# A linear-attention and MLP kernel: seven block products for one more group, 100 unread matmuls at the start, and casts moved between engines

## The chip, the cores and the metric

The kernel runs on one core of a Trainium2 chip. A core has TensorE for matrix products, VectorE, ScalarE and GpSimd for elementwise work, and SyncE (SP), which here only issues transfers. Each engine takes its own instructions in order, and they wait for each other by semaphores. The metric is the device time of one execution in microseconds; less is better.

## The reference

Two layers follow each other. The first is attention with a decaying state, in blocks of 64 positions, for 4 sequences of 768 positions and 8 heads of 64. Its output is normalised and goes through an MLP with a residual:

```python
for b in range(nb):
    intra = np.einsum('bhic,bhjc->bhij', qb, kb) * Dmask[None]
    intra = np.einsum('bhij,bhjd->bhid', intra, vb)
    inter = np.einsum('bhid,bhde->bhie', qb * lam_pow[None], kv_state)
    out[:, :, sl] = intra + inter
    kv_state = lam_block * kv_state + np.einsum('bhsd,bhse->bhde', kb * rev_pow[None], vb)
...
xn = (x - mu) / np.sqrt(var + 1e-06) * g_ln
ch = np.maximum(xn @ w_ch1, 0.0) @ w_ch2          # 512 -> 2048 -> 512
return (x + ch).astype(np.float32)
```

## The kernel before

The 3072 positions are cut into 12 units of 256, each a pair of two chunks of 128 of one sequence. Units 0 to 3 are the first 256 positions of the four sequences, 4 to 7 the next, 8 to 11 the last. Unit u has its attention, and then the MLP for its two tiles of 128 positions, which make group u. The order of all work is written out by hand at the end of the kernel: the attention's steps are called by name, and between them `units(n)` takes the next n pieces of MLP work from a list, `plan`. A piece of the first layer (`m1`, line 530) is eight 128x256 matmuls.

Input stage. `load_in` and `load_window` issue the transfers of k, q and v on SP, `load_w1` and `load_w2` those of the weights, in four pieces each, on GpSimd's queue. `behind` (line 727) makes GpSimd read one column of a tile, so that the weight transfers issued after it start only when that tile has landed; in the same way `open_in(u, True)` writes one column of k's buffer on GpSimd ahead of that unit's loads. `in_k` and `in_k_one` cast k to bf16, `in_q` and `in_q_one` scale q, `in_v` scales v; each call names its engine. The transposes of k and q are TensorE's (`transpose_pe`, line 250) for units 0 to 2 and transfers (`transpose_dma`, line 257) for the later ones.

Attention. `scores` and `mask` make the masked products of k and q, `kv` the state products pk0 and pk1 in PSUM (line 307), `new_state` adds the old state on VectorE (`Stmp`, line 317) and multiplies by the decay on GpSimd (`Sn`, line 313), `av` and `inter` sum the output in PSUM. `s1` is `kv`, `scores`, `new_state` and `mask` together; `s2` is the second half of the scores; `X1` and `X2` are the like for the later units. `reader` (line 443) copies eight columns of the output's PSUM as a fence between the two halves of `inter`; the constant WG decides its engine. `norm` takes the mean and makes xc; g_row in it is the norm's weight, which one matmul with a row of ones (`g_all`, line 180) spreads over 128 partitions. `to_xT` transposes xc.

Second layer. For groups below WG = 4 it is the plain product (`m2`, line 666): for each of two tiles 16 matmuls of 128x512. For groups from WG on it is a scheme with seven products in place of eight (`m2.w`, line 565): the operands are cut 2 x 2, sums of blocks are made beforehand, and each product is eight matmuls of 128x256. The weights' block sums `wt` are made once (`w_sums(c, n)`, two VectorE operations for each half n of piece c, 16 in all), those of the hidden layer for each group (`sums`, lines 548 to 550, six VectorE operations). The products accumulate in four PSUM tiles, a to d, taken from the same four buffers ("mm") as pm1, pk0 and pk1:

```python
        products = (("P1", "a", True), ("P2", "b", True), ("P7", "c", True), ("P5", "d", True),
                    ("P6", "a", False), ("P4", "c", False), ("P3", "d", False))
```

`evict` takes them out: P1 and P7 through ScalarE (`ev_u`, `ev_p`) and an add on GpSimd (lines 590 and 598), the others on VectorE (line 578). Each `m2.w` piece is seven matmuls, so that a group's second layer is eight pieces either way.

Of the kernel before, what the change touches and what calls it, by code (L numbers as in the profile page):

```python
# [7 lines left out]
F32 = mybir.dt.float32  # L8
BF16 = mybir.dt.bfloat16
# [8 lines left out]
def kernel(  # L18
# [11 lines left out]
    nc = tc.nc  # L30
# [11 lines left out]
    NWC = 4  # L42
    eps = 1e-6
    XS = 64.0
    WG = 4
    assert D == 64 and S % W == 0 and DM == 512

    ctx.enter_context(tc.manual_schedule())
# [1 line left out]
    const = ctx.enter_context(tc.tile_pool(name="const", bufs=1))  # L50
# [4 lines left out]
    ps = ctx.enter_context(tc.tile_pool(name="ps", bufs=1, space=PSUM))  # L55
# [16 lines left out]
    def fill(got, name, u, hs, eng=None):  # L72
        eng = eng or nc.sync
        src = dict(k=k, q=q, v=v)[name]
        if u < LB:
            eng.dma_start(got[:, hs], source(src, u, hs))
            return
        cc, b = divmod(u, B)
        for j in range(2):
            eng.dma_start(got[:, hs, j * D:(j + 1) * D],  # L80
                          src[b, hs, cc * W + j * C:cc * W + (j + 1) * C, :].rearrange("h p d -> p h d"))
# [11 lines left out]
    def load_in(u, name, eng):  # L93
        got = qkv_in[u][name]
        fill(got, name, u, slice(0, H), eng)
        qkv_in[u][name] = got.rearrange("p h (j d) -> p h j d", j=2)
# [28 lines left out]
    g_row = const.tile([128, DM], F32)  # L125
    g_one = wk.tile([1, DM], F32, tag="xc", name="g_one")
    nc.scalar.dma_start(g_one, moe_g_ln[None, :])


    ident = const.tile([128, 128], BF16)  # L130
# [20 lines left out]
    def make_keep64():  # L151
        for dst, base in ((keep64, 0), (keep64_b, D)):
            nc.gpsimd.memset(dst, 1.0)
            nc.gpsimd.affine_select(
                out=dst, in_=dst, compare_op=ALU.is_ge, fill=0.0,
                base=base, pattern=[[1, D]], channel_multiplier=-1,
            )
        nc.vector.tensor_copy(keep64[half[1]], keep64_b[half[1]])
# [18 lines left out]
    ones = const.tile([1, 128], F32)  # L177
    nc.vector.memset(ones, 1.0)
    g_all = ps.tile([128, DM], F32, tag="po1", name="g_all")
    nc.tensor.matmul(g_all, lhsT=ones, rhs=g_one, start=True, stop=True)  # L180

    lnlam = const.tile([128, H], F32)
# [15 lines left out]
    def open_window(u):  # L198
        kq = wk.tile([128, 2, NP, 2, 2, D], BF16, tag="kq", bufs=3, name="kq")
        vb = wk.tile([128, H, 2, D], BF16, tag="vb", bufs=4, name="vb")  # L200
        st[u] = dict(kq=kq, vb=vb)
        if u < XB:
            st[u]["kqT"] = wk.tile([128, 2, NP, 2, 128], BF16, tag="kqT", bufs=3, name="kqT")

    def part(a, dst, hs):

        return dst[:, a, hs.start // 2:hs.stop // 2].rearrange("p a j e d -> p a e j d")
# [3 lines left out]
    def in_k(u, eng, hs=ALL):  # L211
        src = qkv_in[u]["k"][:, hs].rearrange("p (a e) j d -> p a e j d", e=2)
        dst = part(0, st[u]["kq"], hs)
        for j in range(2):
            (eng.copy if eng is nc.scalar else eng.tensor_copy)(dst[:, :, :, j], src[:, :, :, j])
# [13 lines left out]
    def in_k_one(u, eng, j):  # L229
        src = qkv_in[u]["k"].rearrange("p (a e) j d -> p a e j d", e=2)  # L230
        (eng.copy if eng is nc.scalar else eng.tensor_copy)(part(0, st[u]["kq"], ALL)[:, :, :, j], src[:, :, :, j])

    def in_q_one(u, eng, j):
        src = qkv_in[u]["q"].rearrange("p (a e) j d -> p a e j d", e=2)
        lq = (lam_q[:, :, j] if u < LB else lam_p[:, 0, :]).rearrange("p (a e) -> p a e", e=2)
        eng.tensor_tensor(part(1, st[u]["kq"], ALL)[:, :, :, j], src[:, :, :, j],  # L236
                          lq[:, :, :, None].to_broadcast([128, NP, 2, D]), op=ALU.mult)
# [22 lines left out]
    def scores(u, hf, early=False):  # L260

        s = st[u]
        kT, qT = s["kqT"][:, 0], s["kqT"][:, 1]
        if early:
            sc = [mm_tile([128, 2, 2, 128], F32, f"sce{e}") for e in range(2)]
        else:
            sc = [ps.tile([128, 2, 2, 128], F32, tag="sc", bufs=2, name=f"sc{e}") for e in range(2)]
        mA = wk.tile([128, 2, 2, 2, 128], BF16, tag=f"mA{hf}", name=f"mA{hf}")
        for i in range(2):
            for jk in range(2):  # L270
                for ab in range(2):
                    for e in range(2):
                        nc.tensor.matmul(sc[e][half[ab], i, jk, :], lhsT=kT[half[e], 2 * hf + i, jk, half[ab]],  # L273
                                         rhs=qT[half[e], 2 * hf + i, :, half[ab]],
                                         start=(i == 0 and jk == 0), stop=(i == 1 and jk == 1), skip_group_check=True)
        s[f"mA{hf}"] = mA
        s[f"sc{hf}"] = sc

    def mask(u, hf, heads=(0, 1)):
        s = st[u]  # L280
        kp = keep.rearrange("p a b t -> p a (b t)")
        for e in heads:
            nc.vector.tensor_tensor(s[f"mA{hf}"][:, e], s[f"sc{hf}"][e],  # L283
                                    kp[:, None, :, :].to_broadcast([128, 2, 2, 128]), op=ALU.mult)
# [139 lines left out]
    def inter(u, first, fence=True):  # L424


        s = st[u]
        qT = s["kqT"][:, 1]
        todo = [(e, p, ab, jq) for p in range(NP) for jq in range(2)
                for e, ab in ((first, 0), (1 - first, 1)) if s["S"][ab][jq] is not None]  # L430
        for i, (e, p, ab, jq) in enumerate(todo):
            nc.tensor.matmul(s["po"][ab][half[jq], 2 * p + e, :], lhsT=qT[half[e], p, jq, half[ab]],  # L432
                             rhs=s["S"][ab][jq][half[e], p, :],
                             start=False, stop=(first == 1 and i >= len(todo) - 4), skip_group_check=True)
        if first == 0 and fence:
            reader(u)

    def reader(u):
        s = st[u]
        for ab in range(2):  # L440
            if s["S"][ab][1] is not None:
                seen = wk.tile([128, H], F32, tag="seen", name="seen")
                (nc.scalar.copy if u > WG else nc.vector.tensor_copy)(seen, s["po"][ab][:, :, 0])

    def norm(u, ab, early=False):
        s = st[u]
# [66 lines left out]
    m2s = {}  # L513
# [267 lines left out]
    def w_sums(c, n):  # L781
        v = w2[c].rearrange("p (k e) d -> p k e d", e=2)
        w = DM // 2
        b11, b12, b21, b22 = v[:, :, 0, 0:w], v[:, :, 0, w:], v[:, :, 1, 0:w], v[:, :, 1, w:]
        t1, t2, t3, t4 = (wt[c][:, :, i] for i in range(4))
        if n == 0:
            nc.vector.tensor_tensor(t1, b12, b11, op=ALU.subtract)
            nc.vector.tensor_tensor(t3, b12, b22, op=ALU.add)
        else:
            nc.vector.tensor_tensor(t2, b11, t3, op=ALU.subtract)  # L790
            nc.vector.tensor_tensor(t4, t2, b21, op=ALU.add)
# [28 lines left out]
    def s1(u):  # L820
        kv(u)
        scores(u, 0)
        new_state(u, 0, nc.gpsimd)
        mask(u, 0, (0,))
        new_state(u, 1, nc.gpsimd)
        mask(u, 0, (1,))
# [38 lines left out]
    def s2(u):  # L865
        scores(u, 1)
        mask(u, 1)
# [11 lines left out]
    def s4(u):  # L879
        inter(u, 1)  # L880
        if st[u]["S"][0][1] is not None:
            norm(u, 0)
        norm(u, 1)
# [55 lines left out]


    open_window(1)
    in_k(1, nc.scalar)
    norm(0, 0, early=True)
    reader(0)
    behind(qkv_in[1]["k"][:, 0, 0, 0:1])
# [72 lines left out]
    for g in range(2, len(groups)):  # L1018
        m1, m2 = mlp(g)
        plan += [(m1, n) for n in range(m1.count)]  # L1020
        if g >= WG:
            plan += [(m2.w, n) for n in range(8)]
# [5 lines left out]
    def units(n):  # L1028
        for _ in range(n):
            f, *a = next(steps)  # L1030
            f(*a)
# [15 lines left out]
    s3(2)  # L1047
    units(2)
    s4(2)
    open_window(3)  # L1050
    in_k_one(3, nc.vector, 0)
    in_k_one(3, nc.vector, 1)
    in_q_one(3, nc.gpsimd, 0)
    in_q_one(3, nc.gpsimd, 1)
    in_v(3, nc.gpsimd)
# [10 lines left out]
    units(1)  # L1066
    load_in(5, "v", nc.sync)
    units(1)
    open_window(4)
    in_k_one(4, nc.gpsimd, 0)  # L1070
    in_k_one(4, nc.gpsimd, 1)
# [1 line left out]
    in_q_one(4, nc.gpsimd, 1)  # L1073
    in_v(4, nc.gpsimd)
    units(5)
    w_sums(0, 0)
    w_sums(0, 1)
    units(2)
    w_sums(1, 0)
    units(1)  # L1080
    s1(3)
    store(0)
    transpose_dma(4, 0)
    transpose_dma(4, 1)
    units(2)
    s2(3)
    units(1)
    open_window(5)
    in_k_one(5, nc.gpsimd, 0)
# [8 lines left out]
    open_in(6, False)  # L1098
    load_in(6, "k", nc.sync)
    units(1)  # L1100
    load_in(6, "q", nc.sync)
    units(1)
    w_sums(1, 1)
    load_in(6, "v", nc.sync)
    units(1)
    w_sums(2, 0)
    transpose_dma(5, 0)
    units(1)
    make_keep64()
    to_xT(3, 0)  # L1110
    transpose_dma(5, 1)
    open_in(7, False)
    load_in(7, "k", nc.sync)
    units(1)
    w_sums(2, 1)
    s1(4)
    to_xT(3, 1)
    open_window(6)
# [7 lines left out]
    units(2)  # L1126
    s3(4)
    units(1)
    in_q_one(6, nc.vector, 1)
    in_v(6, nc.gpsimd)  # L1130
    s4(4)
    in_q_one(6, nc.vector, 0)
    units(3)
    load_in(7, "q", nc.sync)
    units(1)
    w_sums(3, 0)
    w_sums(3, 1)
    units(1)
    open_in(8, False)
    to_xT(4, 0)  # L1140
# [216 lines left out]
```

## Time and profile before

| | us |
|---|---|
| median of 7 runs | 210.84 |
| lowest and highest | 209.77, 212.53 |
| the profiled execution | 209.77 |
| its span, first to last instruction | 208.1 |

| engine | busy, us | share of the span |
|---|---|---|
| TensorE | 198.1 | 95% |
| VectorE | 137.7 | 66% |
| ScalarE | 120.0 | 58% |
| GpSimd | 84.8 | 41% |

The profile is one execution; its instructions carry start and length, the line of the kernel, the tiles written and read, and, in brackets, how long the engine was idle before and what ended that. PE is TensorE, PEld its weight loads, DVE VectorE, ACT ScalarE, POOL GpSimd. The ends of matmuls are modelled, so that in a stream their starts, or the chain that ended last, tell the pace. A row "x16" is sixteen instructions merged, with the time from the first start to the last end. The granted clock in this profile is 1.00 throughout. The program moves 36.39 MB by transfers, at a mean of 175 GB/s.

### The profile page before, as it was taken

What the parts mean: (1) busy time and instruction counts of PE and PEld (TensorE: products, weight loads), DVE (VectorE), ACT (ScalarE), POOL (GpSimd) and SP (SyncE); (2) the same over time, 40 slices, a digit from 0 to 9 for tenths busy, and PEclk for the clock granted to TensorE, in tenths of its full rate; (3) what the DMA queues carried; (4) which work ended last, traced back from release to release, by engine and by line L of the source; (5) the groups of instructions that cost most, each with busy time, mean ns of one, the idle gap of its engine ahead of it and who ended that gap; (6) DMA issues with size and microseconds to landing.
All of it is one profiled execution on the core that took longest, in us unless ns stands there. A gap on an engine that the chain in (4) does not pass through costs nothing.

```text
span 208.1 us, 7231 instructions
## 1 busy us (share of the span) xinstructions
PE 198.1 (95%) x3099; PEld 156.1 (75%) x3099; DVE 137.7 (66%) x277; ACT 120.0 (58%) x277; POOL 84.8 (41%) x116
## 2 busy tenths in 40 slices
PE   2989999999999999999999999999999999999992
PEld 0468788555775587488888888888888888988881
DVE  2677570529565767767888776676877947865253
ACT  3865769235354667357566775585596565652620
POOL 4649138239556330635365441782282202011020
PEclk9999999999999999999999999999999999999999
DMA  4999999999999988984897999798957020178403
GB/s 109 299 269 217 209 298 168 226 305 263 194 317 191 217 188 160 194 249 78 184 212 116 189 199 167 198 217 129 230 107 175 3 50 3 25 144 274 119 14 88
DMA packets 91042, 36.39 MB, mean 175 GB/s; under 512 B 65153, under 2 KB 88193, under 8 KB 91010
## 3 DMA queue, kind: packets, MB, share of 16 engines
q1 hardware_dynamic: 86400, 31.53, 72.3%
q0 software_dynamic: 4224, 4.19, 12.5%
q8 instruction: 24, 0.39, 0.8%
q10 hardware_dynamic: 386, 0.20, 0.4%
q14 instruction: 8, 0.07, 0.1%
HBM read 27.27 MB, written 6.29 MB: 161 GB/s over the span
## 4 chain that ended last, share of the span: by engine, by line
PE 78%; issue 7%; DVE 5%; ACT 4%; DMA 3%; POOL 1%; SPq 1%; POOLq 0%; ACTq 0%; DVEq 0%
PE pm L530 31%; PE pm L666 14%; PE pwa L565 5%; PE pwd L565 5%; PE pwc L565 5%; PE pwb L565 3%; PE pm1t L640 2%; PE po L419 2%; PE po L432 2%; DMA out_dram<-x 2%; PE sc L273 1%; DMA g_one<-in_moe_g_ln_dram 1%; PE tp L250 1%; PE xt L493 1%; DVE x L578 1%
## 5 line engine op out<-in xcount | busy, mean ns | idle before, releaser
L530 PE MATMUL pm<-xT,w 128*128 128x256 bf16 x736 | 84.8, 273 | 0.0
L530 PEld LDWEIGHTS <-w 128*128 128x128 bf16 x736 | 70.5, 98 | 9.5 <-DVE Smid L388 0.3
L533 ACT ACTIVATE hT<-pm 128x512 f16<-128x512 f32 x92 | 53.9, 600 | 29.2 <-PE pm L530 29.1
L666 PE MATMUL pm<-w,hT 128*128 128x512 f16 x128 | 30.2, 380 | 0.0
L565 PEld LDWEIGHTS <-hs 128*128 128x128 f16 x256 | 24.9, 98 | 2.9
L313 POOL TENSOR_TENSOR Sn<-Stmp,lam_s 128x256 bf16<-128x256 f32 x16 | 9.8, 616 | 39.1 <-DVE Stmp L317 21.0
L590 POOL TENSOR_TENSOR x<-ev_u,x 128x256 f32<-128x256 f32 x8 | 6.4, 796 | 46.4 <-ACT ev_u L589 46.4
L548 DVE TENSOR_TENSOR hs<-hT 128x1024 f16<-128x1024 f16 x16 | 13.8, 864 | 16.5 <-ACT hT L533 16.5
L565 PEld LDWEIGHTS <-hT 128*128 128x128 f16 x192 | 18.1, 98 | 3.6 <-ACT hT L533 1.6
L666 PEld LDWEIGHTS <-hT 128*128 128x128 f16 x128 | 11.7, 98 | 12.1
L283 DVE TENSOR_TENSOR mA<-sc,keep 128x512 bf16<-128x512 f32 x20 | 13.1, 685 | 6.6 <-PE sc L273 6.6
L458 ACT ACTIVATE x<-po 128x512 f32<-128x512 f32 x18 | 10.6, 591 | 9.8 <-PE po L419 5.5
L460 DVE SCALAR_TENSOR_TENSOR xc<-po,nmean,g_row 128x512 bf16<-128x512 f32 x18 | 13.0, 746 | 4.5 <-ACT nmean L459 4.4
L503 ACT ACTIVATE sq<-x,nmean 128x512 bf16<-128x512 f32 x18 | 13.0, 721 | 0.3
L578 DVE SCALAR_TENSOR_TENSOR x<-pwd,rstd,x 128x256 f32<-128x256 f32 x16 | 7.7, 483 | 8.0 <-POOL x L598 8.0
L236 POOL TENSOR_TENSOR kq<-qin,lam_q 128x512 bf16<-128x512 f32 x10 | 10.3, 1045 | 6.1 <-DMA qin<-in_q_dram 6.1
L242 POOL TENSOR_TENSOR vb<-vin,lam_p 128x1024 bf16<-128x1024 f32 x6 | 11.4, 1897 | 2.2 <-DMA vin<-in_v_dram 2.2
L242 POOL TENSOR_TENSOR vb<-vin,lam_v 128x1024 bf16<-128x1024 f32 (+1 forms) x7 | 11.8, 1687 | 1.1 <-DMA vin<-in_v_dram 1.1
L550 DVE TENSOR_TENSOR hs<-hs,hT 128x512 f16<-128x512 f16 x16 | 10.1, 628 | 0.6
L494 ACT COPY xT<-xt 128x512 bf16<-128x512 bf16 x10 | 5.8, 584 | 7.7 <-PE xt L493 7.7
L236 POOL TENSOR_TENSOR kq<-qin,lam_p 128x512 bf16<-128x512 f32 x9 | 9.3, 1043 | 1.5 <-DMA qin<-in_q_dram 1.5
L597 ACT ACTIVATE ev_p<-pwc,rstd 128x256 f32<-128x256 f32 x8 | 3.8, 476 | 10.2 <-PE pwc L565 10.2
(129 smaller groups left out, 305.0 us busy)
## 6 DMA issues: line engine op xcount, KB each, us to landing
out_dram<-x SPq DMA_DIRECT2D x22, 256.0 KB, 3.9
w<-in_moe_w_ch_dram POOLq DMA_DIRECT2D x8, 512.0 KB, 8.7
kin<-in_k_dram SPq DMA_DIRECT2D x14, 256.0 KB, 5.2
qin<-in_q_dram SPq DMA_DIRECT2D x14, 256.0 KB, 4.9
vin<-in_v_dram SPq DMA_DIRECT2D x14, 256.0 KB, 5.1
kin<-in_k_dram SPq DMA_DIRECT2D x5, 512.0 KB, 7.1
qin<-in_q_dram SPq DMA_DIRECT2D x5, 512.0 KB, 8.4
vin<-in_v_dram SPq DMA_DIRECT2D x5, 512.0 KB, 8.5
```

The source lines that it names most:

```text
L236: eng.tensor_tensor(part(1, st[u]["kq"], ALL)[:, :, :, j], src[:, :, :, j], lq[:, :, :, None].to_broadcast([128, NP, 2, D]), op=ALU.mult)
L242: eng.tensor_tensor(st[u]["vb"][:, hs], qkv_in[u]["v"][:, hs], lv.to_broadcast([128, n, 2, D]), op=ALU.mult)
L283: nc.vector.tensor_tensor(s[f"mA{hf}"][:, e], s[f"sc{hf}"][e], kp[:, None, :, :].to_broadcast([128, 2, 2, 128]), op=ALU.mult)
L458: nc.scalar.activation(x, po, ACT.Copy, accum_out=sm)
L460: nc.vector.scalar_tensor_tensor(xc, in0=po, scalar=nm, in1=g_row, op0=ALU.add, op1=ALU.mult)
L503: nc.scalar.activation(sq, s["x"][:, ab], ACT.Square, bias=s["nmean"][:, ab:ab + 1], accum_out=ss[:, ab:ab + 1])
L530: nc.tensor.matmul(pm[:, b, :], lhsT=w1[n // W2K][:, kk, (n % W2K) * 128:(n % W2K + 1) * 128], rhs=xT_of[g][:, kk, 0:N], start=(b == 0 and ...
L533: nc.scalar.activation(hT[:, u * NB:(u + 1) * NB, 0:N], pm, ACT.Relu)
L548: nc.vector.tensor_tensor(s13, b[:, :, 1:2, :].to_broadcast([128, n, 2, 128]), b[:, :, 0:4:3, :], op=ALU.subtract)
L550: nc.vector.tensor_tensor(s4, s2, b[:, :, 2], op=ALU.add)
L565: nc.tensor.matmul(pr[bank], lhsT=lhs(r), rhs=rhs, start=(first and r == 0), stop=(r == KB // 2 - 1), skip_group_check=True)
L666: nc.tensor.matmul(acc[i], lhsT=hT[:, kk, i * 128:(i + 1) * 128], rhs=w2[kk // W2K][:, kk % W2K, :], start=(kk == 0), stop=(kk == KB - 1))
```

## The change

- WG goes from 4 to 3: group 3 (the fourth pair's) takes the seven products. The engine of `reader` no longer follows WG: it is ScalarE from unit 3 on, where it was from unit 5 on.
- A tile of zeros, `fill_in`, is set by VectorE as its first instruction, and 100 matmuls of it with itself (8 columns onto 8 partitions, each with its weight load) stand on TensorE ahead of `g_all`. Nothing reads their output.
- The cast of unit 1's k goes from ScalarE to GpSimd, where it stands ahead of `behind` and of the issue of two weight pieces.
- The cast of unit 3's k goes from VectorE to ScalarE, the scaling of unit 6's q from VectorE to GpSimd.
- The eight calls of `w_sums` are spread over earlier places in the order, since group 3 needs all of them, and group 3 gets its two calls of `sums`.

```diff
-    WG = 4
+    WG = 3
...
+    fill_in = const.tile([128, 8], BF16)
+    nc.vector.memset(fill_in, 0.0)
...
     g_all = ps.tile([128, DM], F32, tag="po1", name="g_all")
+    fill_ps = ps.tile([128, 8], F32, tag="po0", name="idle")
+    for _ in range(100):
+        nc.tensor.matmul(fill_ps[0:8], lhsT=fill_in, rhs=fill_in, start=True, stop=True)
     nc.tensor.matmul(g_all, lhsT=ones, rhs=g_one, start=True, stop=True)
...
-                (nc.scalar.copy if u > WG else nc.vector.tensor_copy)(seen, s["po"][ab][:, :, 0])
+                (nc.scalar.copy if u > 2 else nc.vector.tensor_copy)(seen, s["po"][ab][:, :, 0])
...
     open_window(1)
-    in_k(1, nc.scalar)
+    in_k(1, nc.gpsimd)
...
     s4(2)
+    w_sums(0, 0)
     open_window(3)
-    in_k_one(3, nc.vector, 0)
-    in_k_one(3, nc.vector, 1)
+    in_k_one(3, nc.scalar, 0)
+    in_k_one(3, nc.scalar, 1)
...
     load_in(5, "v", nc.sync)
     units(1)
+    w_sums(0, 1)
     open_window(4)
...
     units(5)
-    w_sums(0, 0)
-    w_sums(0, 1)
-    units(2)
     w_sums(1, 0)
-    units(1)
+    w_sums(1, 1)
+    units(3)
     s1(3)
...
     s2(3)
+    w_sums(2, 0)
     units(1)
     open_window(5)
...
     load_in(6, "k", nc.sync)
     units(1)
+    w_sums(2, 1)
     load_in(6, "q", nc.sync)
     units(1)
-    w_sums(1, 1)
     load_in(6, "v", nc.sync)
     units(1)
-    w_sums(2, 0)
+    w_sums(3, 0)
     transpose_dma(5, 0)
     units(1)
+    w_sums(3, 1)
     make_keep64()
...
     units(1)
-    w_sums(2, 1)
     s1(4)
...
-    in_q_one(6, nc.vector, 1)
+    in_q_one(6, nc.gpsimd, 1)
     in_v(6, nc.gpsimd)
     s4(4)
-    in_q_one(6, nc.vector, 0)
-    units(3)
+    in_q_one(6, nc.gpsimd, 0)
+    units(1)
+    m2s[3].sums(0, 4)
+    units(2)
     load_in(7, "q", nc.sync)
     units(1)
-    w_sums(3, 0)
-    w_sums(3, 1)
+    m2s[3].sums(4, 8)
     units(1)
     open_in(8, False)
     to_xT(4, 0)
```

## The prediction

> **What bounds the kernel now.** I read the busy digits first, then the chain that ended last, then the timeline of the stages that the change touches. From the page, the header and two rows of the 40 slices:
>
> ```profile
> span 208.1 us, 7231 instructions
> PE   2989999999999999999999999999999999999992
> DMA  4999999999999988984897999798957020178403
> ```
>
> TensorE is full from about 30 us to the end; the transfers are full from 5 to about 75 us. The chain says what TensorE's time is made of (start, length, what):
>
> ```profile
> 37.61 0.86 PE pm L666 x4
> ...
> 48.84 5.18 PE pm L666 x24
> ...
> 98.63 0.87 PE pwb L565 x8
> 99.51 0.87 PE pwc L565 x8
> ```
>
> In a stream, a 128x512 matmul of the plain second product costs 5.18/24 = 216 ns, a 128x256 one of the seven block products 0.87/8 = 109 ns. Before 30 us it is otherwise. The timeline:
>
> ```profile
> 4.13 2.04 PE L180 MATMUL g_all<-g_one,ones 1*128 1x512 f32 x2 [4.13 <-DMA g_one<-in_moe_g_ln_dram]
> 6.11 0.61 PE L250 MATMUL tp<-ident,kq 128*128 128x128 bf16 x4
> 11.39 0.44 POOL L727 COPY seen_p<-kin 128x1 f32<-128x1 f32 x1 [0.41 <-DMA kin<-in_k_dram]
> 12.49 1.18 ACT L215 CAST kq<-kin 128x512 bf16<-128x512 f32 x2
> 15.84 1.87 PE L640 MATMUL pm1t<-xT,w 128*128 128x128 bf16 x16 [0.32 <-ACT xT L494]
> 18.87 1.05 PE L640 MATMUL pm1t<-xT,w 128*128 128x128 bf16 x16
> 31.86 2.05 POOL L236 TENSOR_TENSOR kq<-qin,lam_q 128x512 bf16<-128x512 f32 x2 [0.82 <-DMA qin<-in_q_dram]
> 33.90 0.63 PE L250 MATMUL tp<-ident,kq 128*128 128x128 bf16 x8
> ```
>
> Two things are to be seen. The same sixteen matmuls take 1.87 us at 15.84 and 1.05 us at 18.87: until about 18 us TensorE runs slow, though the row of the granted clock shows full speed. And at 33.90 the transposes of the third unit's q start as GpSimd ends its scaling (31.86 + 2.05 = 33.91), which began when that q landed. Nothing on TensorE leads to this q: its transfer waited for a GpSimd gate behind the third piece of the first weights (issued at 12.58, 9.9 us to landing, so 22.5), and the gate's other work waits for transfers too. So 33.9 us is a time that TensorE cannot pass however early it comes; behind it TensorE shows next to no idle time up to about 177 us.
>
> **What the Trainium skill says.** "TensorE: Matmul & The Clock Gate", Part 1: the array starts at half clock and goes to full after some 3.4 us of sustained work, in a window that runs free, so that the moment shifts from run to run. The trace agrees: 117 against 66 ns a matmul above. The same page, "Wait — 56ns, not 53.3ns?": a warm matmul takes its columns at 2.4 GHz plus 2.5 ns (the 216 and 109 ns above), and none starts less than 25 ns after the one before; no run here shows the last. "Trainium Architecture — The Big Picture", "What this means for kernel authors": VectorE and GpSimd lock each other out of a shared port. The trace agrees for an operation with two SBUF inputs:
>
> ```profile
> 109.58 1.90 POOL L242 TENSOR_TENSOR vb<-vin,lam_p 128x1024 bf16<-128x1024 f32 x1
> 109.63 2.38 DVE L548 TENSOR_TENSOR hs<-hT 128x1024 f16<-128x1024 f16 x1 [0.75 <-ACT hT L533]
> ```
>
> It takes 0.69 us alone and here ends 0.53 us after GpSimd.
>
> **The change, part by part.**
>
> *Seven products for group 3.* Removed: 32 matmuls at 216 ns = 6.91 us. Added: 56 at 109 ns = 6.11 us. On TensorE, -0.80 us, all of it behind 33.9, where nothing else limits. The price is paid in waits. In the built order of the changed program, the fifth pair's state products (unit 5, s1(5)) come between the second and the third product, and the fourth accumulator takes over the PSUM buffer of pk1, which VectorE frees only with its second Stmp. In before that state product ends at 82.9, and then:
>
> ```profile
> 82.98 0.43 DVE L317 TENSOR_TENSOR Stmp<-pk,Sn 128x256 f32<-128x256 f32 x1 [1.21 <-PE pk L307]
> 83.48 0.61 POOL L313 TENSOR_TENSOR Sn<-Stmp,lam_s 128x256 bf16<-128x256 f32 x1 [7.05 <-DVE Stmp L317]
> 84.13 0.42 DVE L317 TENSOR_TENSOR Stmp<-pk,Sn 128x256 f32<-128x256 f32 x1
> ```
>
> So pk1 is free 1.65 us after the state product ends. TensorE has until then scores 0.35, two matmuls 0.22 and the third product 0.87 = 1.44 us. The fourth waits 0.2 us, plus what GpSimd and VectorE are late: the new GpSimd add of ev_u (0.80) stands ahead of Sn. Its chain: first product ends 1.09 us after the first layer (8 x 0.109 + transposes 0.22), xT copy 0.59, ev_u 0.47, add 0.80: 2.95, against 2.34 + 0.5 for Sn. That is 0.1 us late. Bounds of the wait 0 and 0.7; I take 0.3. Behind the waiting matmul stand only TensorE's own next products. The six sums of this group on VectorE (2 x (0.69 + 0.42 + 0.42) = 3.1 us) take the place of two q scalings (1.22 + 0.68) and four weight sums (1.7) at 76 to 82 us, so they add no load; the last three end at about 82.6, when the first Stmp is due. The evictions grow from two of 0.74 to six on VectorE (3.1 us together), two of 0.47 on ScalarE and two of 0.8 on GpSimd; VectorE is 65% busy from 80 to 90 us and takes the 1.6 us more beside TensorE's work. Net -0.5 (-0.8 to -0.1).
>
> *The weight sums, moved 7 to 15 us earlier, and the operations that make room.* The third pair of casts of k goes to ScalarE (1.1 us from 46.7 on, in an idle time of 1.13; in before VectorE needs 2.63 us there, locked out by GpSimd). The sums at 61.7 stand against GpSimd's scaling and can be locked out up to 3 us; VectorE's next due work is xc at 64.0, used at 67.5, so this is covered. Unit 6's q goes to GpSimd, 2.1 us in gaps (it idles 2.17 before 74.54 and from 76.4 to 83.5). The readers (0.24 us) go to ScalarE, idle there. On SP the transposes of unit 3 come 2 us sooner, and the loads behind them. All nothing; if the cover failed, up to 0.5 us at one place.
>
> *k of the second pair on GpSimd.* From ScalarE go 1.18 us at 12.49; GpSimd gets two casts (about 0.6 us each in its rows) from 11.4, when that k lands. Queued behind them: the gate copy and the issues of two weight pieces, 1.2 us later, then q's scaling, which waits for its q until 15.7 anyway. The transfers are saturated, so what the weights lose there the q and v gain; the pieces land at 20.0 and 22.5 in either order. The transposes that read this k come earlier, but the first pair's transposes behind them wait for xc at 14.73. So no gain; a loss of up to 0.6 us if GpSimd's cast holds up the two masks at 11.36 on VectorE.
>
> *100 unread matmuls.* They start at about 1.0 us, after a VectorE memset, in a stretch where TensorE waits until 4.13. Each has its own weight load. Not shown in before; bounds: 25 ns (the skill's floor), which is 2.5 us and hidden wholly, and 70 ns, 7 us. I take 35 ns: ended at 4.5, the spread of the norm weight 0.4 us late. If they count as work for the clock gate, TensorE is fast from 5 to 8 us on: the slow rows before 18 us (g_all 2.04, transposes, scores, pm1t 1.87) make up some 7 us on the chain, of which half could go, less the ScalarE and VectorE steps between. That is 2 to 3 us at 18 us, but weights land at 20.0 and 22.5, v's scaling ends at 21.2, and then comes 33.9. Against the profiled run, -0.1. It is worth more against runs in which the clock came later: half of up to 3.4 us.
>
> **Sum.** Profiled execution 209.77 (span 208.1 and 1.7 around it): -0.5 - 0.1 = 209.2. That execution was the fastest of seven (median 210.84, up to 212.53). I read their spread as the moving window; if it is gone, the runs lie a little over the sum: 209.4, which is 0.7% under the median. One per cent, 2.1 us, is about what this kernel's measurement tells from no change.
>
> **Rivals.**
> 1. Forecast (50%): clock early, q's landing at 31.8 decides, products gain 0.5: 209.4, own range 208.6 to 210.4.
> 2. The fill does nothing to the clock (20%): eight columns on eight rows of output are little work, and in before TensorE was busy from 9 to 13 us without getting fast. Then the spread stays: median 210.84 - 0.5 = 210.3.
> 3. The early stage yields more (17%): transfers land about 1 us sooner, as the weights no longer compete with the second pair's q and v, and the fourth product does not wait: 209.77 - 0.8 - 1.0 = 208.0. Against it: the transfers' share is full, so bytes decide.
> 4. The fill is too long (13%), ending on the other side. Place: the wait of g_all, which the first transposes at 6.11 stand behind. At 70 ns it ends at 8.0, g_all at 10.0, and sixteen slow transposes (1.7) at 11.7 instead of 9.3: 2.5 us later, with no early clock to repay it: 209.77 + 2.5 - 0.5 = 211.8, and 212.8 against the median. It decides from 36 ns a pair on with a slow clock (0.5 us late). For it: each pair loads weights. Against it: pairs of 64x64 tiles run at 32 ns slow (32 in 1.02 us at 10.43).
>
> **Chances.** Faster by over 1% (under 208.7): case 3 and the lower edge of 1, 0.27. Slower by over 1% (over 212.9): the longer half of case 4 and unseen waits, 0.12. Within: 0.61. The range 208.0 to 211.8 reaches from case 3 to the middle of case 4.
>
> **What would show it.** In the trace after: the fill's rows with their length, ended by 4.5 to 5; pm1t's first sixteen at about 1.05 us; the transposes of unit 2's q still at 33.9, now with an idle gap before them; seven rows of 0.87 in group 3, and a gap of 0.2 to 0.5 before its fourth product. Wrong: pm1t still at 1.87 (case 2), q's landing before 31 us (case 3), g_all ending after 8 us (case 4), or idle time on TensorE after 34 us elsewhere than at the fourth product.

## The result, and the profile after

| | before | after |
|---|---|---|
| median, us | 210.48 (61 runs) | 212.64 (24 runs) |
| lowest and highest | 209.53, 213.26 | 210.69, 215.70 |
| profiled execution | 209.77 | 211.05 |
| its span | 208.1 | 209.3 |

The ratio of after to before is 1.0067, 95% interval 1.0043 to 1.0090: slower by 0.7%, where 0.7% faster was forecast. The ratio leaves out the slow executions, of after the six from 214.19 to 215.70 us with a mean granted clock of 0.987 to 0.992, while the medians of the table take in all. Both profiled executions are among the faster ones of their kernel, and the spans differ by 1.28 us. First the page of after, its header, and the row of TensorE over the 40 slices:

```profile
span 209.3 us, 7497 instructions
PE   6889899999999999999999999999999999999992
```

TensorE starts earlier (6 in the first slice, where it was 2), which is the unread matmuls, and then has three eights in the next four slices, where before has one. The timeline of the start says how far the steps of the prediction came true (start, length, engine, line, what, and in brackets the idle time before and what ended it):

```profile
0.99 2.65 PE L184 MATMUL idle<-fill_in 128*8 128x8 bf16 x100 [0.99 <-DVE eps_t L166]
4.27 2.04 PE L185 MATMUL g_all<-g_one,ones 1*128 1x512 f32 x2 [0.63 <-DMA g_one<-in_moe_g_ln_dram]
13.27 1.17 POOL L220 CAST kq<-kin 128x512 bf16<-128x512 f32 x2 [1.36 <-DMA kin<-in_k_dram]
14.51 1.56 POOL L117 DMA_DIRECT2D w<-in_moe_w_ch_dram  x2
16.64 1.86 PE L645 MATMUL pm1t<-xT,w 128*128 128x128 bf16 x16 [0.32 <-ACT xT L499]
19.67 1.05 PE L645 MATMUL pm1t<-xT,w 128*128 128x128 bf16 x16
26.47 0.19 PE L437 MATMUL po<-Sn,kqT 64*64 64x64 bf16 x1 [0.97 <-issue]
33.48 2.05 POOL L241 TENSOR_TENSOR kq<-qin,lam_q 128x512 bf16<-128x512 f32 x2 [1.68 <-DMA qin<-in_q_dram]
35.22 0.93 PE L255 MATMUL tp<-ident,kq 128*128 128x128 bf16 x8
```

The unread matmuls cost nothing where they stand: 2.65 us for a hundred, ended at 3.6, and `g_all` still waits 0.63 us for its row. They do nothing to the clock: the first sixteen pm1t take 1.86 us (1.87 before). But the second unit's k is cast from 13.27, where it landed at 11.33 before, and pm1t is 0.80 us late. At 26.47 TensorE was idle for 0.97 us with no other reason than "issue"; in before the like is 0.43:

```profile
24.85 0.35 PE L419 MATMUL po<-vb,mA 64*64 64x64 bf16 x21 [0.43 <-issue]
```

At 29.0 before, 30.37 after, TensorE is 1.32 us behind, and the third unit's q, whose landing was to be the fixed floor, lands at 33.4 and not at 31.8, so that most of its transposes wait until 35.58 and not 33.90. Behind them TensorE is 1.62 us late, 0.30 more than ahead of them.

The chain of waits of after leads back from these transposes to that k: k's transfer until 13.22, its cast, the issue of the weight piece at 15.32, which lands at 23.42, the issue of q at 24.20, which lands at 33.40. The experiments tell whether a late link at its head is what makes the end late.

The seven products of group 3, in the timeline of after (the third, the fourth, and what the fourth waits for):

```profile
83.76 0.45 PE L312 MATMUL pk<-vb,kq 64*64 64x64 bf16 x32
83.92 0.80 POOL L595 TENSOR_TENSOR x<-ev_u,x 128x256 f32<-128x256 f32 x1 [5.56 <-ACT ev_u L594]
84.26 0.42 DVE L322 TENSOR_TENSOR Stmp<-pk,Sn 128x256 f32<-128x256 f32 x1
84.74 1.03 PE L570 MATMUL pwc<-wt,hs 128*128 128x256 f16 x8
84.77 0.61 POOL L318 TENSOR_TENSOR Sn<-Stmp,lam_s 128x256 bf16<-128x256 f32 x1
85.42 0.42 DVE L322 TENSOR_TENSOR Stmp<-pk,Sn 128x256 f32<-128x256 f32 x1
85.90 1.05 PE L570 MATMUL pwd<-wt,hs 128*128 128x256 f16 x8
```

From the chains, the second layer of group 3 begins at 81.86 (80.38 before) and the next group's first layer at 91.27 (89.95): 1.48 us late ahead of it, 1.32 behind it. So group 3 gave back 0.16 us of the 0.80, and the loss of this execution was there before it.

### The profile page after: what moved, and what is told of

Read it like the earlier page. It is cut to its first block, busy times and chain, and to the rows that moved or that the text cites. A ratio compares the mean times of both kernels' runs of the same rounds, so it can differ in the third digit from the quotient of the medians.

```text
span 209.3 us, 7497 instructions
## 1 busy us (share of the span) xinstructions
PE 200.4 (96%) x3223; PEld 160.7 (77%) x3223; DVE 142.9 (68%) x281; ACT 121.4 (58%) x282; POOL 90.1 (43%) x122
## 4 chain that ended last, share of the span: by engine, by line
PE 67%; DMA 13%; issue 7%; DVE 4%; POOL 3%; SPq 3%; ACT 1%; POOLq 0%; DVEq 0%
PE pm L535 29%; PE pm L671 10%; PE pwa L570 6%; PE pwd L570 6%; PE pwc L570 5%; DMA qin<-in_q_dram 4%; DMA w<-in_moe_w_ch_dram 4%; DMA kin<-in_k_dram 4%; PE pwb L570 3%; SPq L76 2%; DMA out_dram<-x 1%; PE po L437 1%; PE po L424 1%; DVE x L583 1%; PE po L411 1%
## 5 line engine op out<-in xcount | busy, mean ns | idle before, releaser
L535 PEld LDWEIGHTS <-w 128*128 128x128 bf16 x736 | 70.4, 98 | 10.6 <-issue 1.2
L570 PEld LDWEIGHTS <-hs 128*128 128x128 f16 x288 | 27.8, 98 | 3.9 <-DVE Stmp L322 0.4
L595 POOL TENSOR_TENSOR x<-ev_u,x 128x256 f32<-128x256 f32 x9 | 7.1, 791 | 52.0 <-ACT ev_u L594 52.0
L553 DVE TENSOR_TENSOR hs<-hT 128x1024 f16<-128x1024 f16 x18 | 15.2, 844 | 16.5 <-ACT hT L538 16.5
L570 PEld LDWEIGHTS <-hT 128*128 128x128 f16 x216 | 20.4, 98 | 3.9 <-ACT hT L538 1.6
L671 PE MATMUL pm<-w,hT 128*128 128x512 f16 x96 | 22.6, 380 | 0.0
L463 ACT ACTIVATE x<-po 128x512 f32<-128x512 f32 x18 | 10.6, 591 | 9.5 <-PE po L424 5.3
L671 PEld LDWEIGHTS <-hT 128*128 128x128 f16 x96 | 8.7, 98 | 9.1
L583 DVE SCALAR_TENSOR_TENSOR x<-pwd,rstd,x 128x256 f32<-128x256 f32 x18 | 8.7, 482 | 8.5 <-POOL x L603 8.5
L241 POOL TENSOR_TENSOR kq<-qin,lam_p 128x512 bf16<-128x512 f32 x11 | 11.3, 1043 | 1.5 <-DMA qin<-in_q_dram 1.5
L247 POOL TENSOR_TENSOR vb<-vin,lam_p 128x1024 bf16<-128x1024 f32 x6 | 11.4, 1896 | 0.5 <-DMA vin<-in_v_dram 0.5
L555 DVE TENSOR_TENSOR hs<-hs,hT 128x512 f16<-128x512 f16 x18 | 10.9, 606 | 0.6
L602 ACT ACTIVATE ev_p<-pwc,rstd 128x256 f32<-128x256 f32 x9 | 4.3, 476 | 11.6 <-PE pwc L570 11.6
L583 DVE SCALAR_TENSOR_TENSOR x<-pwa,rstd,x 128x512 f32<-128x512 f32 (+1 forms) x18 | 10.3, 612 | 0.8
```

Source lines behind the costliest of these rows:

```text
L247: eng.tensor_tensor(st[u]["vb"][:, hs], qkv_in[u]["v"][:, hs], lv.to_broadcast([128, n, 2, D]), op=ALU.mult)
L535: nc.tensor.matmul(pm[:, b, :], lhsT=w1[n // W2K][:, kk, (n % W2K) * 128:(n % W2K + 1) * 128], rhs=xT_of[g][:, kk, 0:N], start=(b == 0 and ...
L553: nc.vector.tensor_tensor(s13, b[:, :, 1:2, :].to_broadcast([128, n, 2, 128]), b[:, :, 0:4:3, :], op=ALU.subtract)
L555: nc.vector.tensor_tensor(s4, s2, b[:, :, 2], op=ALU.add)
L570: nc.tensor.matmul(pr[bank], lhsT=lhs(r), rhs=rhs, start=(first and r == 0), stop=(r == KB // 2 - 1), skip_group_check=True)
L583: nc.vector.scalar_tensor_tensor(out, in0=in0, scalar=r[ab], in1=in1, op0=ALU.mult, op1=ALU.add)
```

## The experiments

Each run's ratio is to runs of the kernel before on the same chip; each kernel was profiled in one execution. There were three theories at first. A: the cast of k ahead of the gate delays the weights. B: 200 more TensorE instructions at the start (each matmul has its weight load) disturb the start through the transfers that fetch instructions. C: the products make the loss.

**The parts alone.** Before with the cast:

```diff
-    in_k(1, nc.scalar)
+    in_k(1, nc.gpsimd)
```

> The kernel before with one edit: the cast of the second pair's k on GpSimd. Theory A (the cast stands in GpSimd's queue ahead of the gate and the issue of two weight pieces, so that every later landing moves, and with it the third unit's q, which TensorE waits for at 34 us): the two pieces are issued about 1.2 us later (13.0 and 13.8), the third unit's q lands 1.0 to 1.6 us later than 31.8, the transposes of that q start at 35 to 35.6 instead of 33.9, and the time is 0.5 to 0.8% over before (ratio 1.005 to 1.008). Theory B (the 100 matmuls disturb the start, the cast is harmless): ratio 1.000 to 1.002, q lands at 31.8. Theory C (the landings differ by chance between profiled executions; the loss is made by the seven products): ratio 1.000 to 1.002.

Measured: 1.0023 [1.0009, 1.0037]. The weight issues come at 13.09 and 13.90 (11.77 and 12.58 before), the third q lands at 32.62, 0.83 us later. The cast costs a quarter of a per cent, less than half of what theory A expected. The chain that A names isn't shown. In the kernel with the products alone (below), which has neither the cast nor the fill, the same issue comes at 13.05, because k landed late, at 12.88, and yet the third q lands at 31.54, earlier than in before:

```profile
13.05 1.55 POOL L117 DMA_DIRECT2D w<-in_moe_w_ch_dram  x2
31.62 2.05 POOL L236 TENSOR_TENSOR kq<-qin,lam_q 128x512 bf16<-128x512 f32 x2 [1.16 <-DMA qin<-in_q_dram]
```

Eight of the profiled programs have the same first 47 us, before and all that leave out the cast and unread matmuls. In them the second k lands between 11.3 and 13.4 us, the first gated weight piece between 20.0 (before, the earliest) and 21.4, the third q between 31.5 and 32.5, and at about 28 us six of the seven others are 0.03 to 1.6 us behind before, one 3.6. After's k at 13.2, its weights at 20.9 and its 1.32 us lie inside these ranges; its q at 33.4 does not.

Before with the 100 matmuls:

```diff
+    fill_ps = ps.tile([128, 8], F32, tag="po0", name="idle")
+    for _ in range(100):
+        nc.tensor.matmul(fill_ps[0:8], lhsT=fill_in, rhs=fill_in, start=True, stop=True)
     nc.tensor.matmul(g_all, lhsT=ones, rhs=g_one, start=True, stop=True)
```

> The kernel before with the 100 unread matmuls alone. Theory A: they end before 4.0 us, pm1t's first sixteen still take 1.87 us, nothing moves, ratio 0.999 to 1.002. Theory B: 200 more TensorE instructions have to be fetched by transfers in the first microseconds, which delays k, q and v (second pair's k at 13.2 instead of 11.3), ratio 1.005 to 1.008. Theory C: ratio 1.000.

Measured: 1.0109 [1.0067, 1.0152], more than the whole change. In the profile TensorE is 2.54 us late when the first MLP pieces start and 3.11 at 31 us, and no later at the end (2.99). The second k lands at 15.1 us, later than in any of the eight. The DMA part of the profile between 4 and 9 us has a line that before has not, here of after and then of this kernel (packets, MB, share of 16 DMA engines):

```profile
q8 instruction: 1, 0.02, 1.4%
```

```profile
q8 instruction: 1, 0.02, 1.5%
```

TensorE's instructions come by transfers, in packets of 16,384 bytes (24 in before, 25 in after). The first is fetched at 15.0 us in before, and with the fill at 5.9 (after) and 6.5 (this kernel), among the loads of q, k and v. The Trainium skill has this on "Runtime: NRT & Kernel Launch", section "Instruction fetch mechanics": each engine's stream is refilled in blocks of 16 KiB, 256 instructions, and the cost of a crossing is "mostly hidden". The packets agree with it.

Before with the products and their moved casts and sums:

```diff
-    WG = 4
+    WG = 3
...
+    w_sums(0, 0)
...
+    m2s[3].sums(0, 4)
...
+    m2s[3].sums(4, 8)
```

> The kernel after without the 100 matmuls and with the second pair's k cast on ScalarE as before: only the seven products for group 3, the moved weight sums and what makes room for them. Theory A: TensorE's 0.8 us less, of which the wait of the fourth product takes 0.6 back: ratio 0.998 to 1.000. Theory B: the same. Theory C: ratio 1.005 to 1.008, with waits of TensorE that the profiled execution of after did not show.

Measured: 1.0103 [1.0072, 1.0134], a loss as large as the fill's, which only theory C had expected. In this profile's waits TensorE has a reason that isn't a wait for anybody:

```profile
PE po L432 <- issue: 1.4, 1, 1.4
PE po L419 <- issue: 0.7, 1, 0.7
```

Its timeline shows the first:

```profile
91.75 0.45 PE L353 MATMUL sc<-kqT 64*64 64x64 bf16 x32
92.03 0.27 PE L432 MATMUL po<-Sn,kqT 64*64 64x64 bf16 x11
93.72 0.24 PE L432 MATMUL po<-Sn,kqT 64*64 64x64 bf16 x5 [1.43 <-issue]
```

Sixteen equal matmuls that need the same inputs stop after eleven, and the next starts 1.6 us later. After has no such gap there, although it has the same products.

The change without the cast:

```diff
-    in_k(1, nc.gpsimd)
+    in_k(1, nc.scalar)
```

> The kernel after with one edit undone: the second pair's k cast on ScalarE. Theory A: the loss goes, ratio to before 0.998 to 1.000, the third unit's q lands at 31.8. Theory B: the loss stays, 1.005 to 1.008. Theory C: the loss stays, 1.005 to 1.008.

Measured: 1.0092 [1.0056, 1.0128], against 1.0067 of the whole change: taking the cast back mends nothing that can be seen, and A isn't the main cause. The second k lands at 15.2 us here too.

**Theory D.** Numbering TensorE's instructions in the trace, every one of these "issue" gaps lies at number 193 + 256n, where a block ends. In the products alone they are at 3009 and 3521. The 256 instructions before 3009 are 16 MLP matmuls of 128x256 and some 112 attention matmuls of 64x64, with their weight loads, and take 2.9 us, where 128 MLP matmuls would take 128 x 109 ns = 14 us. From the starts in the instruction records and the transfer records:

| kernel, block from us | lasts | its successor's fetch starts | next block starts after that | gap |
|---|---|---|---|---|
| before, 19.9 | 4.99 | 2.68 later | 2.30 | 0.62 |
| after, 21.1 | 5.39 | 3.09 | 2.30 | 1.16 |
| products alone, 89.2 | 4.54 | 2.34 | 2.20 | 1.62 |
| products alone, 104.9 | 4.68 | 2.11 | 2.58 | 0.72 |
| products alone, 82.8 (a block without a gap) | 6.37 | 2.38 | 3.99 | 0.00 |

The fetch starts 2 to 3 us into a block, and what it fetched runs 2.2 to 2.6 us after that. A block that TensorE gets through in less than the sum ends in a gap, where the fetch begins inside it. It needn't: in after the block from 160.5 us lasts 4.04 us without a gap, and the fetch of its successor had begun at 159.7, in the block before. What starts a fetch the runs don't show. The products bring 24 matmuls more, 48 instructions, and shift all later code by that much against the block ends: on to two dense steps. In after, the fill's 200 make it 248, nearly a whole block, and the dense steps lie as before.

So theory D: the number of instructions ahead of a dense step, not what they do, decides. Theory E against it: the products and the waits about them cost the time. First the shift without the products, before with 24 unread matmuls:

```diff
+    for _ in range(24):
+        nc.tensor.matmul(fill_ps[0:8], lhsT=fill_in, rhs=fill_in, start=True, stop=True)
```

> The kernel before with 24 of the unread tiny matmuls (128x8 outputs) at its start: 48 more TensorE instructions, the same number by which the seven block products shift all later code, and no products changed. Theory D (the instruction stream comes in blocks of 256 instructions by transfers; a dense attention step in which one block is spent in less than about 4.5 us leaves TensorE idle with nothing else to wait for): the landings stay as before (third q at 31.8, no early block of instructions between 4 and 9 us), gaps ended by 'issue' of 0.7 to 2 us near 91 and 107 us, ratio 1.006 to 1.011. Theory E (the loss of the kernel with the products alone is made by the products and the waits about them): no such gaps, ratio 0.999 to 1.001.

Measured: 1.0134 [1.0069, 1.0198]. The timeline stops at the same matmul:

```profile
93.64 0.45 PE L358 MATMUL sc<-kqT 64*64 64x64 bf16 x32
93.92 0.27 PE L437 MATMUL po<-Sn,kqT 64*64 64x64 bf16 x11
95.60 0.25 PE L437 MATMUL po<-Sn,kqT 64*64 64x64 bf16 x5 [1.41 <-issue]
```

The gaps are 1.61 us at number 3009 and 0.78 at 3521, those of the products alone within 0.06 us, without any product. This shows D for these two gaps, and E falls for them. They are some 2.3 us of the 4.1 that this span is longer; the rest was there by 77 us: the third q was late as well, 33.0, with no early fetch, and TensorE's clock was slow until 24.0 us in that execution.

Then work of the full array in few instructions:

```diff
+    fill_ps = ps.tile([128, 512], F32, tag="po0", name="idle")
+    for _ in range(7):
+        nc.tensor.matmul(fill_ps, lhsT=fill_in[:, 0:128], rhs=fill_in, start=True, stop=True)
```

> The change whole, but with 7 unread matmuls of 128x512 outputs and 128 weight columns in place of the 100 of 128x8: 14 more instructions instead of 200. Theory D: no block of instructions is fetched between 4 and 9 us, the first q, v and k land as in the kernel before (second k at 11 to 12 instead of 13.2), the third q lands at 31.5 to 32.6; ratio 0.997 to 1.002 unless the shifted blocks (62 instructions) fall into a dense step again, which would cost up to 1.9 us (1.009). On the clock: if matmuls that fill the array open TensorE's clock and the tiny ones do not, the first sixteen of pm1t take about 1.05 us instead of 1.86; if the clock opens by elapsed time alone, 1.86 stays. Theory B's rival, that any unread work at the start costs 1%, gives 1.007 to 1.012.

(The kernel is the one before with these seven matmuls and nothing else of the change, not "the change whole".) Measured: 1.0011 [0.9988, 1.0034]. No block is fetched between 4 and 9 us, and the second k lands at 11.4. The weights land at 20.9 and 23.5, as in after, at next to no cost. So unread work at the start is not harmful in itself. It doesn't help either:

```profile
1.26 3.17 PE L184 MATMUL idle<-fill_in 128*128 128x512 bf16 x7 [1.26 <-DVE eps_t L166]
4.36 2.07 PE L185 MATMUL g_all<-g_one,ones 1*128 1x512 f32 x2
16.08 1.87 PE L645 MATMUL pm1t<-xT,w 128*128 128x128 bf16 x16 [0.32 <-ACT xT L499]
```

The shift of 14 instructions left a gap of 0.78 us at number 3009.

Then the products with the dense steps taken apart, so that MLP pieces lie between them:

```diff
-    X1(6)
+    av(5, range(NP))
+    inter(5, 0)
+    units(2)
+    kv64(6)
+    states64(6, 0)
+    states64(6, 1)
...
-    X(7)
-    units(1)
+    av64(6)
+    inter(6, 0)
+    units(1)
+    kv64(7)
+    scores64(7)
+    inter(6, 1)
...
```

> The products alone (no unread matmuls, second pair's k cast by ScalarE), with the attention steps of stages 6 and 7 spread among the units of the other streams, so that no stretch of dense 64x64 matmuls spends a block of instructions in less than 4.5 us. Same instructions, another order. Theory D: the 'issue' gaps of 1.6 and 0.7 us between 90 and 110 us are gone, ratio 0.998 to 1.000. Theory E (the products cost it): 1.008 to 1.012 as without the spread.

Measured: 0.9999 [0.9973, 1.0024], where the same products in the old order gave 1.0103 (median 210.94 us against 212.91). The gaps went from 1.62 and 0.72 to 0.40 and 0.20 us, 1.74 of the 210 us, which is 0.8%.

On top of it the step with pk1 one unit earlier, ahead of the third product's wait:

```diff
     load_in(7, "q", nc.sync)
+    s1(5)
     units(1)
     m2s[3].sums(4, 8)
...
-    s1(5)
```

> The same as the spread kernel, with the step that makes pk1 of stage 5 moved ahead of the unit in which the fourth block product waits, so that the product does not wait for the chain pk1, S, Stmp. Theory D with the wait of 0.64 us as the rest of the loss: the gap before pwd is under 0.2 us, the products' 0.8 us come through in full, ratio 0.995 to 0.998. Theory E: 1.004 to 1.008.

Measured: 0.9987 [0.9961, 1.0012]; pwd now follows pwc without a gap (85.01 after a last part of 0.44 from 84.57). One block still ends in a gap of 0.37 us at 108 us. It is short of the 0.995 to 0.998 that D expected, and not told apart from the kernel before, whose median was 211.30 us on the chip of these four runs and 210.40 to 210.45 on the three others; the medians of the last two are 210.94 and 210.86.

**Towards a faster version.** Here pk1 stands still one unit earlier, and the scores of stage 7 behind the next piece (the second edit, against the last kernel):

```diff
     kv64(7)
-    scores64(7)
     inter(6, 1)
...
     units(1)
+    scores64(7)
+    mask64(7, 0)
+    mask64(7, 1)
```

> The kernel with the products, the spread attention steps and the early pk1, and two more moves: pk1's step one unit earlier still (so that the sums of the second half no longer queue behind its masks on VectorE) and the scores of stage 7 one unit later. Theory D: the 0.16 us wait on hs before the third product and the 0.3 us within the layer of 64 matmuls after 105 us go, ratio 0.995 to 0.998. If the products are worth nothing once the fetch is cured (theory E in its weak form): 0.999 to 1.001.

Measured: 1.0070 [1.0043, 1.0096], a miss. The gap at number 3521 grew from 0.37 to 0.86 us: the move changed which instructions share the block. It is 0.86 of some 1.5 us lost; the rest is open.

The spread without products, twice (the second as its own run), and with the 24 unread matmuls:

> The kernel before with the attention steps of stages 6 and 7 spread and nothing else. If the spread is no gain in itself, only the cure of stalls that the kernel before does not have: ratio 0.999 to 1.001. If it is worth something in itself (the kernel before has one issue gap of 0.4 us near 91): 0.997 to 0.999; then part of what the spread kernels with the products show is the spread's and not the products'.

> The kernel before with 24 unread tiny matmuls at its start (alone 1.013) and the spread of the attention steps of stages 6 and 7. Theory D: the issue gaps of 1.6 and 0.8 us are gone, ratio 0.998 to 1.003. If the 24 matmuls cost their 1.3% in another way than through the dense steps: 1.010 to 1.016.

> The kernel before with the spread alone, once more, since its first profile held a stall of 2 us on a cast at 24 us, ahead of anything the spread moves. If its 0.5% lies behind 88 us: the trace is even with the kernel before up to there and about 1 us later at the end. If it lies in the start: later already at 80 us, ratio anywhere from 0.999 to 1.006.

Measured: 1.0053 [1.0034, 1.0073], 1.0072 [1.0054, 1.0090], 1.0045 [1.0015, 1.0074]. The first two are not where either side was expected. The spread alone leaves no gap over 0.11 us at any block's end after 80 us, and most of its loss lies ahead of all that it moves: TensorE is 3.39 us behind before at 77 us in the first profile and 1.59 in the second, 3.54 and 1.86 at the end. In the second the first differences are these:

```profile
18.84 1.54 PE L640 MATMUL pm1t<-xT,w 128*128 128x128 bf16 x16
21.43 1.05 PE L530 MATMUL pm<-xT,w 128*128 128x256 bf16 x8 [0.48 <-DMA w<-in_moe_w_ch_dram]
23.20 0.45 PE L307 MATMUL pk<-vb,kq 64*64 64x64 bf16 x32 [0.72 <-POOL vb L242]
```

The sixteen matmuls take 1.05 us in before. The trace's own record of TensorE's clock begins, with full speed, at 18.2 us in before and at 19.9 here, and the page counts the time ahead of it as full. Then the first weights landed at 21.4 and 23.9, against 20.0 and 22.5, and the second unit's v was late. In the first profile the pk matmuls waited 1.96 us for that v, and the sixteen behind them, 1.92 us in before, ran in a stretch from 24.5 to 27.9 us for which the trace records half the clock:

```profile
24.61 3.52 PE L530 MATMUL pm<-xT,w 128*128 128x256 bf16 x16
```

The instructions are the same as before's up to 88 us. The time was longer in both runs, so the half per cent may belong to the program; the landings and the clock can't be put down to it, since the other kernels with this start differ among themselves as much, the products with the spread have weights at 21.15 and 23.65 at a ratio of 0.9999, and before was profiled once. What sets them is open. A difference in the start between two profiles of this kernel is thus no evidence by itself, and a ratio here is only worth as much as the gaps that a trace shows beside it. With the 24 matmuls the spread removed the gap at 3009 (1.61 to 0.24) and made the one at 3521 longer (0.78 to 1.56): half a cure.

Last, the pk matmuls of stage 7 some five units ahead:

```diff
+    kv64(7)
+    states64(7, 0)
+    states64(7, 1)
     units(2)
     load_in(8, "q", nc.sync)
```

> The products, the spread of stage 6's attention step, the early pk1, and of stage 7's step the pk matmuls moved some five units ahead, so that the block of instructions that was spent in 4.0 us (with a 0.37 us gap at its end, 108 us) holds 32 more matmuls of 109 ns and lasts some 7 us. Theory D: no gap over 0.2 us at a block's end between 80 and 130 us; ratio 0.995 to 0.998. If the spread itself costs time in another way than by the blocks: 1.000 to 1.006, with no such gap.

Measured: 1.0222 [1.0174, 1.0269], above all that was expected. No block end between 80 and 130 us has a gap over 0.11 us, as D says. But the state products take the buffers of the products' accumulators, and the waits say so:

```profile
PE pwd L565 <- DVE Smid L388: 1.8, 1, 1.8
PE pk L372 <- DVE x L578: 1.3, 1, 1.3
```

The two waits are 3.1 us of the 5.1 that TensorE falls behind over this stretch; after them, from 105.0 to 108.4, the trace records half the clock, and eight matmuls of pwd take 1.89 us (1.04 in before). So it can't tell what the products are worth with no gap left. No version beats the kernel before by more than its interval; the spread with early pk1 beats the change.

## Why the prediction was wrong

*100 unread matmuls "hidden", at -0.1.* This is the step that failed. The sum had them as TensorE's time alone. That was covered: starts 25 ns apart, the least the prediction allowed, 2.65 us in all. The term that decided was not in the sum: the matmuls as instructions. Alone they cost 1.09% [0.67, 1.52], all of it ahead of 31 us, while seven wide ones, which take 3.17 us in 14 instructions, cost 0.11% [-0.12, 0.34]. With the fill and no cast the second k lands at 15.1 and 15.2, against 11.3 to 13.4 in the eight programs without it. In after and with the fill alone the second half of the first v lands at 10.6 and 11.2, in the kernels without the hundred at 9.6 to 10.3. The early fetch is shown; that it, and not another effect of 200 instructions, moves these landings is argued from the seven wide matmuls, which move neither this k nor this v. One packet took 1.08 us in after, about as much as the v was late (0.94). A second term left out is the end of an early block: 1.16 us between two starts in after at 26 us, 1.21 with the fill alone, against 0.62 in before; in two kernels without the fill it was 0.88 and 1.46. How much of after's own 0.7% each makes, one profile doesn't tell.

*The clock early, the runs' spread gone.* This failed too. Of the 1.44 us from 210.84 to the forecast of 209.4 only 0.6 were the change's; the rest was the spread of the runs, which was to go with an early clock. It stayed slow, as rival 2 had it, for tiny matmuls and for full ones, and the runs of after spread from 210.69 to 215.70 us. The Trainium skill's page "TensorE: Matmul & The Clock Gate", Part 1, has the array speed up after about 3.4 us of sustained work, in a window that runs free. The free-running part fits: in the fifteen profiles the clock's record begins at 17.7 to 24.0 us. The 3.4 us doesn't: with the seven wide matmuls TensorE shows no wait over 0.33 us from 1.26 us on (by modelled ends), and the record begins at 19.1; here the measurement decides. (All unread operands are zeros; others were not tried.) The 117 and 66 ns of the prediction contain the modelled end of the last matmul; by their starts the matmuls are 103 and 56 ns apart.

*"The pieces land at 20.0 and 22.5 in either order", "the transposes of unit 2's q still at 33.9".* The time was taken as fixed, from one profile. In after the pieces landed at 20.9 and 23.4 and q at 33.4. The cast alone cost 0.23%, within the loss of up to 0.6 us that was allowed. That a later issue of the pieces makes their landing later is not shown: issued at 13.05 in the products alone they landed at 20.3 and 22.9, issued at 11.6 with the wide matmuls at 20.9 and 23.5. And the late q is the smaller part: TensorE was 1.32 us behind when it came to these transposes and 1.62 after them.

*Seven products, -0.8 and a wait of 0.3.* The sum of durations held: seven rows of 0.87. The wait of the fourth was right: pwc starts at 84.74, eight at 109 ns end at 85.61, pwd starts at 85.90, 0.29 us, by the chain that was named (ev_u's add 0.80, Sn 0.61, Stmp 0.42). pk1 came free 1.63 us after the state product ended (84.21 to 85.84), 1.65 were predicted. Too small was the rest of the sum: the third product waits too, 0.15 us, for pk0's first Stmp (84.68), and the state products at the group's end take 0.47 instead of 0.29 us in the chain. Together they make 0.62 of the 0.64 that are missing. The net is -0.16 where -0.5 was taken, in the bounds given, -0.8 to -0.1. What the prediction didn't see is that 48 instructions more are a cost or none by where they put the block ends: 1.03% in the products alone, nothing in after, where 248 is almost a block.

*The moved sums and casts at no cost.* Nothing in after contradicts it: from the first layer's pieces behind the third unit's transposes (36.15, 34.53 before) to group 3 the lag goes from 1.62 to 1.48 us.

*The rivals.* The other side was given to a fill that takes too long; the fill made the kernel slower by another way, its instructions and not its duration. The chance of 0.12 was for unseen waits as well, and the measured 0.7% is within the one per cent called no change, but the median of 212.64 is above the range.

*How the parts add up.* They don't: 0.23, 1.09 and 1.03% alone, 0.67% together. The shift of the products is undone by the fill's: the two without the cast give 0.92%. That the cast adds nothing to them may be chance; the intervals overlap.

## What to carry to other kernels

Count a change's instructions on a full engine, not only their time: dense stretches of small matmuls can use up the fetched instructions, and a shift of a few dozen moves the gap from one stretch to another. When the engine waits for "issue" in the middle of equal instructions, look where the transfers of instructions start. And a landing read from one profile is no floor: in eight programs with the same start the third q landed between 31.5 and 32.5 us. Profile the unchanged kernel more than once before a change is charged with such a shift.

## What the runs showed of the hardware

- TensorE's instructions come in packets of 16,384 bytes, 256 instructions; one took 0.9 to 2.2 us, half of them under 1.1. Where an "issue" gap of 0.2 us or more was seen at a block's end, the fetch for the next block had begun 1.6 to 3.4 us after the block's start, and the next block began 2.2 to 3.0 us after the fetch; the gaps were 0.2 to 1.6 us. The one profile beyond that is the change without the cast: 4.1 us and a gap of 2.1, in an execution of 214.1 us. The skill's "mostly hidden" holds for most of the 24 crossings of a run and not for those in dense attention steps.
- Matmuls of 8 columns onto 8 partitions, each with its weight load, start 25 ns apart while TensorE's clock is slow, 100 in 2.65 us.
- TensorE worked from 1.26 us on with no wait over 0.33 us by the modelled ends (seven wide matmuls), and the clock became full only at 19.1 us. Over fifteen profiles that moment lies between 17.7 and 24.0 us; 128x128 matmuls start 103 ns apart before it and 56 after.
- After TensorE had waited 1.96 us and 3.1 us for others, the traces record half the clock for 3.4 us (24.5 to 27.9, and 105.0 to 108.4), in two of fifteen profiles.
- Programs with the same first 47 us differ by up to 1.4 us in the landing of the first weights and 2.0 us in that of the second k, in one execution each. Why is open.
